# Random-feature attention followed by an ELU layer on one core: the order of work within a beat, the lags of the ELU steps, a PSUM bank of its own for the second products, a fixed pattern of pieces, and x on VectorE

## The chip, the cores and the metric

The kernel runs on one core of one Trainium2 chip. The metric is the device time of one execution in microseconds, median of three runs.

## The reference

```
# attention: q, k, v (8, 8, 576, 64); w_phi (64, 128)
phi(x):  proj = x @ w_phi;  proj -= max(|proj|)
         return concat(exp(proj), exp(-proj))
kv  = phi(k)^T @ v          z = sum over s of phi(k)
x   = phi(q) @ kv / (phi(q) @ z + 1e-6)
# the 8 heads side by side: x is (4608, 512)
h   = x @ w_in              (512 to 2048)
g   = where(h > 0, h, exp(min(h, 0)) - 1)     # ELU
out = g @ w_out             (2048 to 512)
```

## The kernel before

**Attention.** It is cut into 16 quads of four heads (two quads make a batch). One quad's work is a list of steps: transposes of k and q (`tr`), five projections of k (`k_head`: two matmuls into a PSUM tile `pk`, a maximum `m_k` on VectorE, two exponentials `EK` on ScalarE), five of q (`q_head`, only the maximum `m_q`), the scale and six scaled pieces of v on GpSimd (`vs`), five feature products of q (`pq`, two exponentials `Eq`), two `kv` products with a copy by ScalarE, five output heads (`pn0`, `pn1`, combined on VectorE into `tot`), and x = tot times the reciprocal (`rec`), which DMA transposes turn into `xT`. Both exponentials of a `pk` wait for the maximum of the same tile, since the framework orders readers of one PSUM bank. All these PSUM tiles rotate through one pool, `apsum`, of five banks.

**The ELU layer.** It goes in 9 chunks of 512 rows, each of 32 pieces of four 512-column matmuls: 16 first products `mm1` (w_in times xT into `ph`) and 16 second products `mm2` (four 128-row groups `tt`, each of four parts into one bank `po`, then a copy to `o_sb` on ScalarE and a store). Behind each `mm1` come three steps: `e_sb` = exp(ph) on ScalarE, `u_sb` = e - 1 on GpSimd, and `gT` = max(min(u, 0), ph) on VectorE, which gives the bank of `ph` back. `ph` and `po` rotate through one pool, `mpsum`, of three banks. Chunk c needs the xT of batch c; chunk 8 holds the last 64 rows of every head.

**The order.** From quad 2 on each engine's instruction order is the order of the code. Time is cut into slots of 16 beats, one slot for each quad. A slot n holds the k, q and v steps of quad n, the kv and output steps of quad n-1, and the transposes of quad n+1, at beats written out in `slot_beats`. What a step leaves to another engine is put on an agenda by `post(lag, fn)` and is issued at the start of beat now + lag, in the order in which it was posted. A beat issues its agenda, then the attention steps, then as many pieces as a due time asks for (about 10 in a slot up to slot 5, then 16.34). `moe_piece` takes the first products of a chunk while there are no second ones, so that within a chunk the 16 `mm1` come in a row and then the 16 `mm2`. When first and second products of neighbouring chunks stand ready together, they alternate. Quads 0 and 1 come before the beats, in a fixed list.

Of the kernel before, what the change touches and what calls it, by code (L numbers as in the profile page):

```python
# [22 lines left out]
def kernel(  # L23
# [11 lines left out]
    P = 128  # L35
# [87 lines left out]


    beat = [0]
    agenda = {}
    in_beats = [False]

    def post(lag, fn):
        if in_beats[0]:  # L130
            agenda.setdefault(beat[0] + lag, []).append(fn)
# [11 lines left out]
    def attention_steps(i):  # L143
# [57 lines left out]

        def exps(psum, dst):

            for sg in range(2):
                post(
                    1 + sg,
                    lambda sg=sg: nc.scalar.activation(  # L207
# [4 lines left out]
        def k_head(hh):  # L212
            pk = project(st["kT"], hh, st["m_k"])
            if hh < 4:
                exps(pk, lambda sg: st["EK"][:, hh, sg, :])
            else:
                exps(pk, lambda sg: st["EKt"][:, sg, :])

# [30 lines left out]
        def q_features(par, c):  # L249
# [7 lines left out]
            )  # L257
            exps(pq, lambda sg: st["Eq"][:, par, c, sg, :])

        def q_features_tail():  # L260
            pq = apsum.tile([P, 2, P], FP32, name="pq", tag="ap")
            for c in range(2):
# [6 lines left out]
                )  # L269
            exps(pq.rearrange("p a b -> p (a b)"), lambda sg: st["Eqt"][:, sg, :])  # L270

# [3 lines left out]

            post(2, weights)

        def kv(s):
# [17 lines left out]
            for c in range(2):  # L296
                for sg in range(2):
# [7 lines left out]
                    )  # L305
            post(1, lambda: nc.scalar.copy(st["kv"][:, s], pkv))

# [61 lines left out]
        def divide():  # L369
# [4 lines left out]

            def x_head(c):
                r = slice(c * NS, (c + 1) * NS)
                eng.tensor_tensor(  # L377
                    st["x"][:, :, c, :],
# [3 lines left out]
                )  # L382

            for c in range(2):
                post(1 + c, lambda c=c: x_head(c))

# [40 lines left out]
    def mm1(ch, jt):  # L427
# [3 lines left out]
        for ct in range(N_CT):  # L431
# [8 lines left out]
        u_sb = moesm.tile([P, CHUNK], BF16, name="u_sb")  # L440
        post(1, lambda: nc.scalar.activation(e_sb, ph, ACT.Exp))  # L441
        post(
            1,
            lambda: nc.gpsimd.tensor_scalar(  # L444
                u_sb, e_sb, -1.0, 1.0, op0=ALU.add, op1=ALU.mult
            ),
        )
        post(
            2,
            lambda: nc.vector.scalar_tensor_tensor(  # L450
                gTs[ch][:, jt, :], u_sb, 0.0, ph, op0=ALU.min, op1=ALU.max
            ),
        )

    pos = {}

    def mm2(ch, tt, part):

        if part == 0:
            pos[ch, tt] = mpsum.tile([P, DM], FP32, name="po", tag="mp")  # L460
        po = pos[ch, tt]
# [10 lines left out]
        o_sb = moesm.tile([P, DM], FP32, name="o_sb", bufs=2)  # L472
        post(1, lambda: nc.scalar.copy(o_sb, po))  # L473

# [17 lines left out]

    first, second = [], []
    turn = [0]

    def chunk_ready(ch):
        first.extend((ch, jt) for jt in range(N_JT))

    def moe_piece():
        take_first = first and (  # L500
            not second or (turn[0] == 0 and second[0][0] >= first[0][0] - 1)
        )
        if take_first:
            ch, jt = first.pop(0)
            mm1(ch, jt)
            turn[0] = 1
            if jt == N_JT - 1:

                post(
                    2,  # L510
                    lambda: second.extend(
                        (ch, tt, part)
                        for tt in range(CHUNK // P)
                        for part in range(4)
                    ),
                )
        elif second:
            mm2(*second.pop(0))
            turn[0] = 0

# [7 lines left out]
    def slot_beats(n):  # L528
        at = [[] for _ in range(BEATS)]
        old, new, nxt = quads.get(n - 1), quads.get(n), quads.get(n + 1)  # L530
        if n == 2:
            old = None
        if old:
            at[0] += old["kv"][:1]
            at[1] += old["kv"][1:]
            for t, f in zip((3, 5, 7, 9, 11), old["out"]):
                at[t].append(f)
            at[14].append(lambda: post(1, old["x"][0]))
        if new:
            for t, f in zip((0, 1, 3, 4, 5), new["k"]):  # L540
                at[t].append(f)
            for t, f in zip((2, 6, 8, 10, 12), new["q"]):
                at[t].append(f)
            for t, f in zip((7, 9, 11, 13, 15), new["qf"]):
                at[t].append(f)
            at[6].append(lambda: post(1, new["scale"][0]))
            for t, f in zip((7, 8, 9, 10, 11, 11), new["vs"]):
                at[t].append(lambda f=f: post(1, f))
        if nxt:
            at[3] += nxt["tr"][:1]  # L550
            at[6] += nxt["tr"][1:]
        if n % 2 == 1 and n > 3:
            at[4].append(lambda: chunk_ready((n - 3) // 2))
        return at
# [72 lines left out]
    in_beats[0] = True  # L627
    chunk_ready(0)
    done = 0
    for n in range(2, NQ + 1):  # L630
# [3 lines left out]
        if n % 2 == 0 and n // 2 + 1 < B:  # L634
            nb = n // 2 + 1
            alloc_batch(nb)
            for t, f in zip((2, 4, 6, 8), load_kq(nb)):
                at[t].append(f)
            at[10].append(lambda: load_v(nb))
        for t in range(BEATS):  # L640
            next_beat()
            for f in at[t]:
                f()
            now = n + (t + 1) / BEATS
            due = (now - 2) * 32 / 3.25 if now < 5.25 else 32 + (now - 5.25) * 16.34
            while done < due and (first or second):
                moe_piece()
                done += 1
    chunk_ready(B - 1)
    chunk_ready(B)  # L650
    while first or second or agenda:
        next_beat()
# [31 lines left out]
```

## Time and profile before

| | |
|---|---|
| median of 3 runs | 484.35 us (482.02 to 484.66) |
| the profiled execution's own time | 483.06 us |
| its span, first to last instruction | 481.3 us |
| PE (TensorE) busy | 389.0 us, 81% |
| ACT (ScalarE) busy | 270.1 us, 56% |
| DVE (VectorE) busy | 265.8 us, 55% |
| POOL (GpSimd) busy | 244.6 us, 51% |
| mean granted TensorE clock | 0.946 of full speed |

The profile was taken on an execution of 483.06 us, 1.76 us more than its span. Busy times overlap, and a busy TensorE is not TensorE at its peak, since the ends of pipelined matmuls are modelled: how densely it works is read from the distance between the starts of matmuls. PEld is the weight load, which runs beside the matmuls, SPq the queue from which SyncE issues DMAs.

### The profile page before, as it was taken

How to read it: one execution, taken by the hardware profiler on the slowest of the kernel's cores; microseconds unless marked ns; L12 is line 12 of the kernel's file. 1: busy time of each engine (PE TensorE's matmuls, PEld its weight loads, DVE VectorE, ACT ScalarE, POOL GpSimd, SP SyncE). 2: the span in 40 equal slices, each digit the busy share in tenths (PEclk: the TensorE clock that was granted, in tenths of full speed). 3: DMA queues.
4: the chain of work that ended last, by engine and by line, in shares of the span. 5: the costliest groups of instructions: out<-in, count | busy, mean ns of one | idle time of the engine just before them, and what ended most of it. 6: DMA issues, size and time to landing. Idle time of an engine off the chain costs nothing.

```text
span 481.3 us, 7888 instructions
## 1 busy us (share of the span) xinstructions
PE 389.0 (81%) x2888; PEld 206.3 (43%) x2888; DVE 265.8 (55%) x522; ACT 270.1 (56%) x585; POOL 244.6 (51%) x355
## 2 busy tenths in 40 slices
PE   3575757699598797879788977997799779889996
PEld 2344424355244453445344543554355435334442
DVE  2671644578366646664676457745774674264320
ACT  2942156577465666665765657656766683254421
POOL 8645047196166645746393729571925282254320
PEclk9955787899889999999999999999999999999999
DMA  8899974019913981198318930993035003300023
GB/s 132 164 200 199 194 95 63 0 19 152 229 35 51 153 185 47 34 129 201 71 13 117 233 73 1 102 259 72 1 68 98 23 0 49 91 1 22 23 61 69
DMA packets 93718, 44.88 MB, mean 93 GB/s; under 512 B 62544, under 2 KB 88272, under 8 KB 93680
## 3 DMA queue, kind: packets, MB, share of 16 engines
q1 hardware_dynamic: 65136, 29.57, 29.8%
q0 software_dynamic: 28544, 14.82, 23.6%
q8 instruction: 22, 0.36, 0.3%
q14 instruction: 16, 0.13, 0.1%
HBM read 36.77 MB, written 9.44 MB: 96 GB/s over the span
## 4 chain that ended last, share of the span: by engine, by line
PE 37%; POOL 21%; DVE 15%; issue 15%; DMA 7%; ACT 4%; SPq 1%; POOLq 0%; ACTq 0%; DVEq 0%
PE po L463 21%; POOL u_sb L444 12%; PE ph L432 7%; DVE gT L450 6%; DMA q_b<-in_q_dram 3%; POOL vs L242 3%; PE pk L182 3%; POOL x L377 3%; DMA xT<-x 2%; ACT EK L207 2%; DVE tot L337 2%; DVE tot L331 2%; DVE m_q L192 2%; DVE m_k L192 2%; PE pq L251 2%
## 5 line engine op out<-in xcount | busy, mean ns | idle before, releaser
L444 POOL TENSOR_SCALAR u_sb<-e_sb 128x512 bf16<-128x512 f32 x144 | 88.2, 616 | 159.8 <-ACT e_sb L441 144.5
L432 PE MATMUL ph<-xT,w_in_sb 128*128 128x512 bf16 x512 | 134.8, 393 | 38.9 <-DVE gT L450 32.2
L450 DVE SCALAR_TENSOR_TENSOR gT<-u_sb,ph 128x512 bf16<-128x512 bf16 x144 | 97.0, 683 | 115.9 <-POOL u_sb L444 115.1
L463 PE MATMUL po<-w_out_sb,gT 128*128 128x512 bf16 x576 | 140.9, 379 | 0.0
L441 ACT ACTIVATE e_sb<-ph 128x512 f32<-128x512 f32 x144 | 85.4, 602 | 57.7 <-PE ph L432 55.5
L207 ACT ACTIVATE EK<-pk 128x512 bf16<-128x512 f32 x128 | 70.8, 612 | 61.9 <-DVE m_k L192 61.7
L432 PEld LDWEIGHTS <-w_in_sb 128*128 128x128 bf16 x576 | 57.3, 99 | 108.2 <-issue 60.7
L207 ACT ACTIVATE Eq<-pq 128x512 bf16<-128x512 f32 x128 | 73.0, 610 | 21.1 <-PE pq L251 20.9
L463 PEld LDWEIGHTS <-gT 128*128 128x128 bf16 x576 | 55.6, 98 | 53.9 <-issue 1.5
L242 POOL TENSOR_TENSOR vs<-v_b,em 128x512 bf16<-128x512 f32 (+1 forms) x90 | 73.0, 834 | 0.0
L192 DVE TENSOR_REDUCE m_k<-pk 128x4 f32<-128x512 f32 (+1 forms) x80 | 49.1, 632 | 36.8 <-PE pk L182 36.8
L192 DVE TENSOR_REDUCE m_q<-pk 128x4 f32<-128x512 f32 (+1 forms) x80 | 49.9, 627 | 11.0 <-PE pk L182 10.9
L377 POOL TENSOR_TENSOR x<-tot,rec 128x576 bf16<-128x576 f32 x30 | 34.1, 1148 | 16.7 <-DVE rec L373 16.7
L473 ACT COPY o_sb<-po 128x512 f32<-128x512 f32 x36 | 21.3, 590 | 32.2 <-PE po L463 30.2
L182 PE MATMUL pk<-w_phi_both,kT 128*128 128x256 bf16 x144 | 29.5, 288 | 11.3 <-ACT EK L207 6.5
L182 PE MATMUL pk<-w_phi_both,qT 128*128 128x256 bf16 x144 | 30.4, 288 | 7.3 <-ACT EK L207 3.7
L319 PEld LDWEIGHTS <-Eq 128*128 128x128 bf16 x512 | 27.0, 103 | 20.0 <-issue 8.7
L319 PE MATMUL pn<-kv,Eq 128*128 128x65 bf16 x512 | 30.1, 201 | 5.0 <-DVE m_q L192 1.7
L331 DVE TENSOR_TENSOR tot<-pn,w 128x260 f32<-128x260 f32 x64 | 27.0, 423 | 10.2 <-PE pn L319 10.1
L251 PE MATMUL pq<-qT,w_phi_both 128*128 128x512 bf16 x64 | 25.1, 404 | 5.9 <-DVE tot L331 2.1
L337 DVE TENSOR_TENSOR tot<-tot,pn 128x260 f32<-128x260 f32 x64 | 27.0, 424 | 1.9
L182 PEld LDWEIGHTS <-qT 128*128 128x128 bf16 x144 | 14.4, 102 | 25.4 <-issue 13.5
(62 smaller groups left out, 267.2 us busy)
## 6 DMA issues: line engine op xcount, KB each, us to landing
out_dram<-o_sb SPq DMA_DIRECT2D x32, 256.0 KB, 2.7
v_b<-in_v_dram SPq DMA_DIRECT2D x7, 1024.0 KB, 8.7
k_b<-in_k_dram POOLq DMA_DIRECT2D x7, 512.0 KB, 6.1
q_b<-in_q_dram POOLq DMA_DIRECT2D x7, 512.0 KB, 7.8
w_in_sb<-in_moe_w_in_dram POOLq DMA_DIRECT2D x8, 256.0 KB, 8.6
w_out_sb<-in_moe_w_out_dram POOLq DMA_DIRECT2D x8, 256.0 KB, 12.4
v_b<-in_v_dram POOLq DMA_DIRECT2D x2, 512.0 KB, 7.1
out_dram<-o_sb SPq DMA_DIRECT2D x8, 128.0 KB, 2.3
```

What stands on the lines that cost most here:

```text
L182: nc.tensor.matmul(pk[:, 2 * j:2 * j + 2, :].rearrange("p a b -> p (a b)"), xT[:, 2 * hh + j, :], w_phi_rhs, start=True, stop=True,)
L192: lambda: nc.vector.tensor_reduce(m[:, o:o + NT] if hh < 4 else m[:, NS - 1::NS], pk[:, 0:2 * n, :], axis=AX.X, op=ALU.max, apply_absolute ...
L207: lambda sg=sg: nc.scalar.activation(dst(sg), psum, ACT.Exp, scale=1.0 - 2.0 * sg),
L242: eng.tensor_tensor(st["vs"][:, sg, r, 0:D], kqv[b][2][:, o:o + n * D].rearrange("p (n d) -> p n d", d=D), st["em"][:, sg, r, None].to_bro ...
L319: nc.tensor.matmul(pt[:, t, :], st["Eq"][:, par, c, sg, o:o + P], st["kv"][:, s, c, sg, :], start=True, stop=True,)
L331: nc.vector.tensor_tensor(tot, pn[1], st["w"][:, o:o + NT, None].to_broadcast((P, NT, D1)), op=ALU.mult,)
L377: eng.tensor_tensor(st["x"][:, :, c, :], st["tot"][:, r, 0:D], rec[:, r, None].to_broadcast((P, NS, D)), op=ALU.mult,)
L432: nc.tensor.matmul(ph, w_in_sb[:, ct, jt * P:(jt + 1) * P], xTs[ch][:, ct, :] if ch < B else xT_tail[:, ct // 2, :, ct % 2, :], start=(ct ...
L441: post(1, lambda: nc.scalar.activation(e_sb, ph, ACT.Exp))
L444: lambda: nc.gpsimd.tensor_scalar(u_sb, e_sb, -1.0, 1.0, op0=ALU.add, op1=ALU.mult),
L450: lambda: nc.vector.scalar_tensor_tensor(gTs[ch][:, jt, :], u_sb, 0.0, ph, op0=ALU.min, op1=ALU.max),
L463: nc.tensor.matmul(po, gTs[ch][:, jt, tt * P:(tt + 1) * P], w_out_sb[:, jt, :], start=(jt == 0), stop=(jt == N_JT - 1),)
```

## The change

- An agenda item gets a rank; the items of a beat are issued in the order of rank (ELU exponential and u 0, copies from PSUM 1, maxima 2, gT 3, the rest 5, the scale 7).
- The lags of the ELU steps become 1, 2 and 3 beats for `e_sb`, `u_sb` and `gT` (before 1, 1 and 2). Both exponentials of a k projection are posted two beats on, both of a q feature one (before one and two).
- `apsum` has four banks, `mpsum` three for `ph` alone, and a new pool `opsum` one for `po`.
- The pieces stand in a fixed list, one for each beat, issued before the attention steps: two `mm1`, then one `mm2` of the chunk before (its groups 2 and 3), eight times, then the eight `mm2` of the chunk's groups 0 and 1. In chunk 0 the places of the earlier chunk's pieces are empty. A chunk may begin once it is in `ready`, four beats after the issue of its last DMA transposes.
- The steps stand at other beats. Ahead of the beats, x of quad 0 is transposed before the q features of quad 1, and the transposes of quad 2 move to the end.
- x of every quad is multiplied on VectorE, right behind the reciprocal. Before, GpSimd did it one and two beats later (but for quad 1).

```
-        tc.tile_pool(name="apsum", bufs=5, space=bass.MemoryType.PSUM)
+        tc.tile_pool(name="apsum", bufs=4, space=bass.MemoryType.PSUM)
...
+    opsum = ctx.enter_context(
+        tc.tile_pool(name="opsum", bufs=1, space=bass.MemoryType.PSUM)
+    )
...
-    def post(lag, fn):
+    def post(lag, fn, rank=5):
...
-        for fn in agenda.pop(beat[0], []):
+        for _, fn in sorted(agenda.pop(beat[0], []), key=lambda item: item[0]):
             fn()
...
-            def x_head(c):
+            for c in range(2):
                 r = slice(c * NS, (c + 1) * NS)
-                eng.tensor_tensor(
+                nc.vector.tensor_tensor(
...
-        post(1, lambda: nc.scalar.activation(e_sb, ph, ACT.Exp))
+        post(1, lambda: nc.scalar.activation(e_sb, ph, ACT.Exp), 0)
         post(
-            1,
+            2,
             lambda: nc.gpsimd.tensor_scalar(
...
         post(
-            2,
+            3,
             lambda: nc.vector.scalar_tensor_tensor(
...
-            pos[ch, tt] = mpsum.tile([P, DM], FP32, name="po", tag="mp")
+            pos[ch, tt] = opsum.tile([P, DM], FP32, name="po", tag="op")
...
+    for ch in range(B + 1):
+        late = [(ch - 1, tt, part) for tt in (2, 3) for part in range(4)]
+        for j in range(N_JT // 2):
+            pieces += [(ch, 2 * j), (ch, 2 * j + 1)]
+            pieces.append(late[j] if ch > 0 else None)
+        pieces += [(ch, tt, part) for tt in (0, 1) for part in range(4)]
+    pieces += [(B, tt, part) for tt in (2, 3) for part in range(4)]
...
+        if new:
+            put((0, 2, 3, 5, 6), new["k"])
+            at[8].append(lambda: post(1, new["scale"][0], 7))
+            put((9, 10, 11, 12, 13, 14), [lambda f=f: post(1, f) for f in new["vs"]])
         if old:
+            put((3, 4), old["kv"])
+            put((6, 8, 10, 12, 14), old["out"])
+            at[15].append(lambda: post(1, old["x"][0]))
+            if n % 2 == 0:
+                at[15].append(lambda: post(5, lambda: ready.add(n // 2 - 1)))
         if new:
+            put((8, 10, 12, 14, 15), new["qf"])
+            put((0, 2, 9, 11, 14), new["q"])
         if nxt:
+            put((5, 9), nxt["tr"])
...
-    steps += b["vs"][5:] + b["qf"] + quads[2]["tr"]
-    steps += b["kv"] + a["x"] + b["out"] + b["x"]
+    steps += b["vs"][5:] + a["x"] + b["qf"]
+    steps += b["kv"] + b["out"] + b["x"] + quads[2]["tr"]
```

On ScalarE, at the start of slot 2 (the first beats), the order before is this; the number behind a tile's name tells tiles apart:

```order
L207 ACTIVATE EK_501<-pk_664 128x512
L441 ACTIVATE e_sb_673<-ph_668 128x512
L207 ACTIVATE EK_501<-pk_664 128x512
L207 ACTIVATE EK_501<-pk_679 128x512
L441 ACTIVATE e_sb_687<-ph_682 128x512
L207 ACTIVATE EK_501<-pk_679 128x512
```

At the same place on ScalarE the changed kernel has these rows:

```order
L445 ACTIVATE e_sb_673<-ph_668 128x512
L445 ACTIVATE e_sb_689<-ph_684 128x512
L212 ACTIVATE EK_643<-pk_675 128x512 x2
L445 ACTIVATE e_sb_710<-ph_705 128x512
L212 ACTIVATE EK_643<-pk_695 128x512 x2
```

Each `e_sb` stood between the two exponentials of the k projection of its own beat; now it stands ahead of both, and the k projection whose exponentials follow is a beat older.

On VectorE, in the same beats of slot 2, before:

```order
L192 TENSOR_REDUCE m_k_500<-pk_664 128x4
L450 SCALAR_TENSOR_TENSOR gT_667<-u_sb_674,ph_668 128x512
L192 TENSOR_REDUCE m_k_500<-pk_679 128x4
L450 SCALAR_TENSOR_TENSOR gT_667<-u_sb_688,ph_682 128x512
L192 TENSOR_REDUCE m_q_517<-pk_695 128x4
```

On VectorE in the changed kernel:

```order
L196 TENSOR_REDUCE m_k_642<-pk_675 128x4
L196 TENSOR_REDUCE m_q_659<-pk_678 128x4
L196 TENSOR_REDUCE m_k_642<-pk_695 128x4
L196 TENSOR_REDUCE m_q_659<-pk_698 128x4
L455 SCALAR_TENSOR_TENSOR gT_667<-u_sb_674,ph_668 128x512
L196 TENSOR_REDUCE m_k_642<-pk_712 128x4
L455 SCALAR_TENSOR_TENSOR gT_667<-u_sb_690,ph_684 128x512
```

The first `gT` stood behind one maximum; now four maxima, of two later projections of k and two of q, stand ahead of it.

GpSimd before, at the end of slot 5 (`u_sb` of chunk 1, x of quad 4):

```order
L242 TENSOR_TENSOR vs_1598<-v_b_663,em_1595 128x2x64 x2
L444 TENSOR_SCALAR u_sb_1703<-e_sb_1702 128x512
L377 TENSOR_TENSOR x_1498<-tot_1497,rec_1708 128x9x64
L444 TENSOR_SCALAR u_sb_1724<-e_sb_1723 128x512
L377 TENSOR_TENSOR x_1498<-tot_1497,rec_1708 128x9x64
```

VectorE in the changed kernel, at the end of slot 5, x of quad 4:

```order
L196 TENSOR_REDUCE m_q_1576<-pk_1674 128x2
L365 TENSOR_TENSOR tot_1506<-pnt_1663,w_1406 128x2x65
L371 TENSOR_TENSOR tot_1506<-tot_1506,pnt_1663 128x2x65
L379 TENSOR_SCALAR den_1682<-tot_1506 128x18
L380 RECIPROCAL rec_1683<-den_1682 128x18
L384 TENSOR_TENSOR x_1507<-tot_1506,rec_1683 128x9x64 x2
L455 SCALAR_TENSOR_TENSOR gT_1447<-u_sb_1652,ph_1646 128x512
```

x has left GpSimd, where it stood between two `u_sb`; on VectorE it now stands between the reciprocal and the next `gT`.

## Rows read from the trace of the kernel before

**Rows 1.** Stretch, length, busy time (count) of PE, PEld, DVE, ACT, POOL; PEclk, DMA share, GB/s.

```profile
55.40:130.00 74.60, 55.56 (x419) 29.39 (x418) 42.01 (x79) 45.70 (x102) 37.74 (x53) 0.89 0.67 100
130.00:417.70 287.70, 246.53 (x1934) 130.65 (x1934) 173.38 (x343) 176.85 (x388) 156.67 (x221) 0.99 0.49 88
163.30:179.90 16.60, 16.60 (x147) 9.36 (x146) 8.04 (x18) 11.44 (x27) 8.44 (x11) 1.00 1.04 195
179.90:208.60 28.70, 21.43 (x170) 11.27 (x169) 17.99 (x36) 18.98 (x42) 16.32 (x25) 1.00 0.25 53
```

**Rows 2.** Waits of the engines: us in total, times, longest us.

```profile
DVE gT L450 <- POOL u_sb L444: 115.1, 101, 7.5
...
PE ph L432 <- DVE gT L450: 32.3, 47, 2.0
```

**Rows 3.** Timeline of slot 2: start us, us, engine, instruction, idle before it.

```profile
57.35 0.60 ACT L441 ACTIVATE e_sb<-ph 128x512 f32<-128x512 f32 x1
58.04 0.61 POOL L444 TENSOR_SCALAR u_sb<-e_sb 128x512 bf16<-128x512 f32 x1 [11.28 <-ACT e_sb L441]
58.69 0.69 DVE L450 SCALAR_TENSOR_TENSOR gT<-u_sb,ph 128x512 bf16<-128x512 bf16 x1 [2.15 <-POOL u_sb L444]
59.29 0.68 DVE L192 TENSOR_REDUCE m_k<-pk 128x4 f32<-128x512 f32 x1
60.01 0.60 ACT L207 ACTIVATE EK<-pk 128x512 bf16<-128x512 f32 x1 [1.57 <-DVE m_k L192]
60.50 0.59 ACT L441 ACTIVATE e_sb<-ph 128x512 f32<-128x512 f32 x1
```

**Rows 4.** Timeline of TensorE where only second products run beside attention.

```profile
163.33 1.02 PE L463 MATMUL po<-w_out_sb,gT 128*128 128x512 bf16 x4
164.19 0.41 PE L319 MATMUL pn<-kv,Eq 128*128 128x65 bf16 x8
164.43 0.38 PE L251 MATMUL pq<-qT,w_phi_both 128*128 128x512 bf16 x1
164.65 1.02 PE L463 MATMUL po<-w_out_sb,gT 128*128 128x512 bf16 x4
...
174.34 0.67 PE L286 MATMUL pkv<-vs,EK 128*128 128x65 bf16 x16
...
175.17 0.39 PE L182 MATMUL pk<-w_phi_both,kT 128*128 128x256 bf16 x2
175.40 1.03 PE L463 MATMUL po<-w_out_sb,gT 128*128 128x512 bf16 x4
```

**Rows 5.** Groups by line: busy us, mean ns of one, idle before.

```profile
L306 ACT CAST kv<-pkv 128x260 bf16<-128x260 f32 x32 | 12.3, 396 | 10.0 <-PE pkv L298 9.7
...
L377 DVE TENSOR_TENSOR x<-tot,rec 128x576 bf16<-128x576 f32 x2 | 1.4, 754 | 0.0
```

**Rows 6.** Timeline of GpSimd and VectorE late in slot 4.

```profile
115.75 3.78 POOL L242 TENSOR_TENSOR vs<-v_b,em 128x512 bf16<-128x512 f32 x5
...
116.87 1.99 DVE L372 TENSOR_SCALAR den<-tot 128x18 f32<-128x18 f32 x1
```

**Rows 7.** Timeline of the last stretch, chunks 7 and 8.

```profile
424.09 2.75 PE L432 MATMUL ph<-xT,w_in_sb 128*128 128x512 bf16 x12 [0.44 <-DVE gT L450]
...
442.02 1.03 PE L432 MATMUL ph<-xT_tail,w_in_sb 128*128 128x512 bf16 x4
442.22 0.58 ACT L473 COPY o_sb<-po 128x512 f32<-128x512 f32 x1 [0.21 <-PE po L463]
...
475.69 1.03 PE L463 MATMUL po<-w_out_sb,gT 128*128 128x512 bf16 x4
```

**Rows 8.** Timeline of the opening, ahead of the beats.

```profile
36.02 0.27 DVE L373 RECIPROCAL rec<-den 128x18 f32<-128x18 f32 x1
...
42.12 1.03 PE L156 MATMUL tr<-ident,q_b 128*128 128x128 bf16 x8 [2.67 <-DMA q_b<-in_q_dram]
```

**Rows 9.** Timeline of TensorE at the start of chunk 1.

```profile
130.46 2.72 PE L432 MATMUL ph<-xT,w_in_sb 128*128 128x512 bf16 x6 [4.85 <-DMA xT<-x]
```

More of the change, by code (lines that the diff above doesn't have):

```diff
@@ L127 @@
     in_beats = [False]
-    def post(lag, fn):
+    def post(lag, fn, rank=5):
         if in_beats[0]:
-            agenda.setdefault(beat[0] + lag, []).append(fn)
+            agenda.setdefault(beat[0] + lag, []).append((rank, fn))
         else:
@@ L198, in project, with exps @@
                 ),
+                2,
             )
             return pk[:, 0:2 * n, :].rearrange("p a b -> p (a b)")
-        def exps(psum, dst):
+        def exps(psum, dst, lag):
             for sg in range(2):
                 post(
-                    1 + sg,
+                    lag,
                     lambda sg=sg: nc.scalar.activation(
@@ L214, in k_head @@
             if hh < 4:
-                exps(pk, lambda sg: st["EK"][:, hh, sg, :])
+                exps(pk, lambda sg: st["EK"][:, hh, sg, :], 2)
             else:
-                exps(pk, lambda sg: st["EKt"][:, sg, :])
+                exps(pk, lambda sg: st["EKt"][:, sg, :], 2)
         def q_head(hh):
@@ L257, in q_features @@
             )
-            exps(pq, lambda sg: st["Eq"][:, par, c, sg, :])
+            exps(pq, lambda sg: st["Eq"][:, par, c, sg, :], 1)
         def q_features_tail():
@@ L269, in q_features_tail @@
                 )
-            exps(pq.rearrange("p a b -> p (a b)"), lambda sg: st["Eqt"][:, sg, :])
+            exps(
+                pq.rearrange("p a b -> p (a b)"), lambda sg: st["Eqt"][:, sg, :], 1
+            )
             def weights():
@@ L274, in weights @@
                 nc.scalar.activation(st["w"], st["m_q"], ACT.Exp, scale=2.0)
-            post(2, weights)
+            post(2, weights, 6)
         def kv(s):
@@ L305, in kv @@
                     )
-            post(1, lambda: nc.scalar.copy(st["kv"][:, s], pkv))
+            post(1, lambda: nc.scalar.copy(st["kv"][:, s], pkv), 1)
         def out_head(hh):
@@ L382, in x_head @@
                 )
-            for c in range(2):
-                post(1 + c, lambda c=c: x_head(c))
         def x_out():
@@ L440, in mm1 @@
         u_sb = moesm.tile([P, CHUNK], BF16, name="u_sb")
-        post(1, lambda: nc.scalar.activation(e_sb, ph, ACT.Exp))
+        post(1, lambda: nc.scalar.activation(e_sb, ph, ACT.Exp), 0)
         post(
-            1,
+            2,
             lambda: nc.gpsimd.tensor_scalar(
@@ L446, in mm1 @@
             ),
+            0,
         )
         post(
-            2,
+            3,
             lambda: nc.vector.scalar_tensor_tensor(
@@ L452, in mm1 @@
             ),
+            3,
         )
@@ L472, in mm2 @@
         o_sb = moesm.tile([P, DM], FP32, name="o_sb", bufs=2)
-        post(1, lambda: nc.scalar.copy(o_sb, po))
+        post(1, lambda: nc.scalar.copy(o_sb, po), 1)
         def store():
@@ L489, in mm2 @@
         post(2, store)
[L493 to L497, printed above, removed]
-    def moe_piece():
[L500 to L519, printed above, removed]
+    ready = set()
+    pieces = []
+    for ch in range(B + 1):
[5 more added lines that the diff above has]
+    pieces += [(B, tt, part) for tt in (2, 3) for part in range(4)]
+    def moe_piece():
+        if not pieces or (pieces[0] and pieces[0][0] not in ready):
+            return
+        piece = pieces.pop(0)
+        if piece:
+            (mm1 if len(piece) == 2 else mm2)(*piece)
     quads = {}
@@ L532, in slot_beats, with put @@
             old = None
-        if old:
[L534 to L538, printed above, removed]
-        if new:
[L540 to L548, printed above, removed]
+        def put(beats, fs):
+            for t, f in zip(beats, fs):
+                at[t].append(f)
+        if new:
+            put((0, 2, 3, 5, 6), new["k"])
+            at[8].append(lambda: post(1, new["scale"][0], 7))
+            put((9, 10, 11, 12, 13, 14), [lambda f=f: post(1, f) for f in new["vs"]])
+        if old:
+            put((3, 4), old["kv"])
[3 more added lines that the diff above has]
+                at[15].append(lambda: post(5, lambda: ready.add(n // 2 - 1)))
+        if new:
+            put((8, 10, 12, 14, 15), new["qf"])
+            put((0, 2, 9, 11, 14), new["q"])
         if nxt:
[L550 to L553, printed above, removed]
+            put((5, 9), nxt["tr"])
         return at
@@ L627 @@
     in_beats[0] = True
-    chunk_ready(0)
-    done = 0
+    ready.add(0)
     for n in range(2, NQ + 1):
@@ L636 @@
             alloc_batch(nb)
-            for t, f in zip((2, 4, 6, 8), load_kq(nb)):
+            for t, f in zip((4, 5, 6, 7), load_kq(nb)):
                 at[t].append(f)
-            at[10].append(lambda: load_v(nb))
+            at[6].append(lambda: load_v(nb))
         for t in range(BEATS):
             next_beat()
+            moe_piece()
             for f in at[t]:
                 f()
[L644 to L651, printed above, removed]
+    while pieces or agenda:
+        if B - 1 in ready:
+            ready.add(B)
         next_beat()
```

## The prediction

> **What bounds the kernel now.** I read the busy time by stretch first. Between 130.0 us, where chunk 1 begins to flow, and 417.7 us, where chunk 7 does, six chunks pass in 287.7 us, 47.95 us each [rows 1]. No engine is full there: PE 246.5, ACT 176.9, DVE 173.4 us. Within one chunk there are two regimes. In the 16.6 us from 163.3, which hold only second products, PE is busy throughout at full clock; in the 28.7 us from 179.9, which hold the 16 first products, it is busy 21.4 [rows 1]. So PE does not limit a chunk, the first products do.
>
> The waits say by what: DVE waits 115.1 us for u_sb, and PE 32.3 us, in 47 waits, for a gT to give a bank of ph back [rows 2]. The timeline of slot 2 shows why no one is full [rows 3]. An e_sb starts at 57.35, its u_sb at 58.04, its gT at 58.69; only behind that gT may DVE take the maximum of the next k projection (59.29), only behind that maximum may ACT start its exponentials (60.01), and the next e_sb stands behind the first of these (60.50). That is a ring through three engines, 3.15 us a turn, one first product per turn, where PE's own work for such a product is 0.86. In the drain nothing else runs, but three banks for ph are too few for a run of first products alone: after every twelve matmuls PE waits 0.44 [rows 7].
>
> **What the changed order leaves as PE's own work.** The prices come from the stretch in which PE never waits, as distances between starts [rows 4]. A piece of four matmuls takes 0.86 (163.33 to 164.19), an output head 0.24, a q feature 0.22, a kv product 0.83 (174.34 to 175.17), two projection matmuls 0.23. A quad has two kv products (1.66), four heads and a tail counted as one (1.20), 18 projection matmuls (2.07), four features and a small one (0.99): 5.9 us. A chunk has 32 pieces and spans two slots, so 27.6 + 11.8 = 39.4 us. The other engines: DVE spent 173.4 / 6 = 28.9 per chunk and gets the two x, 3.0 more, so 31.9; ACT stays at 29.5. Both are under 39.4, so PE can become the bound if the order lets it.
>
> **Ranks, lags and pattern.** With e_sb first in its beat, u_sb one beat later and gT two beats later behind the maxima, no step waits in its queue behind another that waits for it: the ring is open. I walked one pair of slots beat by beat with the prices above and those of the other engines: an exponential or e_sb starts 0.49 behind the last one (60.01 to 60.50), a gT holds DVE 0.60 (58.69 to 59.29) [rows 3]. What is left per chunk:
>
> Four banks in apsum: the second kv product takes the bank of the second k projection, whose exponentials are issued in the same beat on ACT, behind the copy of the first kv product (mean 0.396 [rows 5]). The copy and two exponentials need about 1.55 with their hand-overs, the piece that hides them is 0.86: PE waits 0.7 in each slot, with all its later work behind, 1.4. Likewise one pn tile waits for the last k exponentials, 0.3 a slot, 0.6.
>
> One bank for po: PE may start the next row group only after the copy. At 442.02 the next product started, the copy at 442.22, for 0.58 [rows 7]; with a hand-over back 0.85. Before, that cost nothing, since two more banks covered it. Of a chunk's four group changes two have other pieces between, two do not; there 0.1 to 0.2 of attention hides some: 1.4.
>
> x on DVE: 0.754 each, two per quad [rows 5]. On GpSimd it stood between u_sb. On DVE it stands in beat 15 behind den and rec, and ahead of a gT. A maximum (0.35), combines, den and rec (1.1), both x (1.5) and that gT (0.6) make some 3.7 us after beat 14; PE needs the gT's bank after 2.3 (a piece, 0.11, a piece, 0.44). PE waits 1.5 there, in one of the two slots of a chunk; in the other slot no first product follows.
>
> The ph ring itself: three banks, but of each three pieces only two take one, so a bank is due back after four pieces, 3.44. The measured turn is 3.19 (2.75 + 0.44 [rows 7]), so no wait in the drain; among the maxima I count 0.4 per chunk.
>
> One more for x: a den, an operation on 18 columns, took 1.99 us while five GpSimd multiplications ran in a row [rows 6]; the reciprocal of the same 18 columns takes 0.27 [rows 8]. So some DVE instructions stand still while GpSimd runs. For x, bounds are 0 (GpSimd idle just then) and one whole GpSimd instruction for each, two times 1.0. I take 0.8 per chunk, a u_sb and a bit, since by beat 15 the long vs pieces are done.
>
> The rule of the Trainium skill for this is in "SBUF — State Buffer", section "Who interferes with whom": a VectorE instruction with two SBUF inputs, as this multiplication has, and a GpSimd instruction that reads SBUF exclude each other for a whole instruction. The den agrees, though no row shows it for x beside GpSimd. By that rule the upper bound holds, and a chunk loses 2.1 instead of 0.8.
>
> Sum: 39.4 + 1.4 + 0.6 + 1.4 + 1.5 + 0.4 + 0.8 = 45.5 us per chunk. The sixth chunk spans slot 16, which has no new quad: it lacks 3.1 of PE's work and 1.0 of the waits, 41.4. Six chunks: 5 x 45.5 + 41.4 = 268.9, against 287.7.
>
> The DMA issues of k and q on GpSimd move from beats 2 to 8 into 4 to 7; they stand between u_sb that have a beat to spare, which hides them. Without that beat each of the four would hold a u_sb, and a gT, for its length. On SP the transposes of q now stand behind the load of v: rival (b).
>
> **The opening.** Before, PE stood in the fixed list in front of transposes that wait for q_b (2.67 idle at 42.12 [rows 8]), with kv, x and the outputs of quad 1 behind them. These transposes move to the end. But now x of quad 0 stands ahead of quad 1's q features: rec starts at 36.02 [rows 8], x ends at 37.8, and transposes, features, ten exponentials and kv follow one another, so that quad 1's outputs begin near 45 and the end of the list comes near 55. I count no gain: 55.4 stays.
>
> From 55.4 to chunk 1 it took 74.6 us, with the ring at its worst and the clock at 0.89 [rows 1]. Now chunk 0 has one beat per piece. Slot 2: 11 first products and three us of attention, PE 12.5, and ACT 27 exponentials of 0.49 plus small ones, 15; I take 17. Slot 3: 13 pieces and 5.9 are 17.1, with 1.8 of the waits above 19. Slot 4 and the first four beats of slot 5 hold no piece at all. Slot 4 is then bound by DVE and ACT, 10 to 12, and by a clock that may fall: I take 15. Until chunk 1 flows another 8.5 pass, since its xT leaves only at the end of slot 4; before, PE waited 4.85 for it [rows 9]. Together 59.5: chunk 1 at 114.9.
>
> **The drain.** Before, 63.6 us from 417.7 to the end of the span, 481.3, with 64 pieces. Now the last eight pieces of chunk 6 are mixed in: 72 x 0.86 = 61.9. Nothing hides the po copies: six group changes of 0.85, 5.1. Behind the last product, which ends near 476.55 (475.69 + 0.86 [rows 7]), copy and store took 4.75 and will again. 71.8, that is 8.2 more.
>
> **The sum.** 114.9 + 268.9 + 71.8 = 455.6 us of span. The profiled execution was 483.06, 1.76 above its span: 457.4. The median shown is 1.29 above that execution, so I predict 459 us, 5% faster.
>
> **Rivals.** (a) *The period stays.* If waits that I don't see take what the open ring frees, a chunk keeps 47.95: 114.9 + 287.7 + 71.8, with the same additions 477.5. For it: in the dense stretch of 16.6 us there are no ELU steps, so no row shows PE and ELU dense together beside attention. Against: DVE and ACT have over 7 us to spare in each chunk. Chance 0.10.
>
> (b) *DMA becomes the bound.* Loads for the next batch now go out in four beats of even slots, and the transposes of q behind them must land before beat 0 of the next slot. At chunk 1 PE waited 4.85 for a transpose [rows 9], in a window that moved 195 GB/s the DMA share was 1.04 [rows 1]. Three us lost in each of six even slots: 477. Chance 0.10.
>
> (c) *x and GpSimd exclude each other fully.* 1.3 more per chunk, 8 in all: 467. The den of 1.99 [rows 6] shows that it can be. Chance 0.08.
>
> (d) *Slower: the short rings.* Four banks for attention, 26 tiles a slot, and PE in order: if three more tiles per slot wait for exponentials of their own beat as the second kv product does, at 0.7 each, 14 slots lose 29 us: 488. The gain is gone from 2.6 such tiles on. For it: the dense stretch that gave the prices [rows 4] ran with five banks. Against: by the walk most tiles have two beats between release and need. Chance 0.09.
>
> (e) *The clock falls in the empty stretch* of 20 beats and chunk 0 runs at 1.2 GHz as it partly does now (0.89 granted): 5 to 8 us, 465. Chance 0.05.
>
> The forecast keeps 0.58; its own range is 449 to 468. The range that leaves out no more than 2 in 10 reaches to (a) and (b): 447 to 479. About 0.5% is what a measurement of this kernel can tell from no change: faster 0.87, same 0.04, slower 0.09.
>
> **What would show it.** Right: starts of first products of neighbouring chunks 44 to 47 us apart; DVE's wait for u_sb below half of 115.1; waits of PE for o_sb near 0.6 to 0.9, some 20 in number; a wait of PE for gT in the beats behind an x; the first ph of chunk 1 near 115; drain near 72. Wrong: PE waits for DMA in even slots (b); x of well over 0.754 (c); frequent waits of PE for ACT exponentials (d); a low clock in slot 4 (e).

## The result and the profile after

The changed kernel takes 445.49 us (median of 4 runs, 444.58 to 447.8) against 483.19 (4 runs, 482.02 to 484.66). The ratio is 0.923, 95% interval 0.918 to 0.928: 7.7% faster, where 5% was predicted. 445.49 lies 1.5 us under the predicted range. The profiled execution took 446.22 us, its span is 444.4.

Busy time by stretch, with the same columns as [rows 1]: from the first beat to chunk 1, inside that slot 4 and the lead to chunk 1, then the six chunks, one steady chunk, and the drain.

```profile
55.09:113.75 58.66, 44.90 (x355) 24.88 (x354) 42.19 (x80) 40.66 (x93) 33.04 (x49) 0.88 0.81 117
92.06:106.70 14.64, 9.73 (x107) 5.93 (x105) 11.32 (x24) 10.56 (x27) 5.63 (x8) 0.82 1.22 206
106.70:113.75 7.05, 3.70 (x30) 2.42 (x30) 5.56 (x11) 2.20 (x6) 1.19 (x3) 0.50 0.94 125
113.75:372.19 258.44, 238.88 (x1964) 129.60 (x1963) 189.57 (x370) 176.81 (x394) 132.31 (x197) 1.00 0.56 96
247.58:291.11 43.53, 40.51 (x342) 22.26 (x339) 33.04 (x64) 31.22 (x72) 24.31 (x36) 1.00 0.68 122
372.19:444.40 72.21, 63.45 (x289) 28.04 (x287) 22.02 (x32) 25.54 (x43) 19.75 (x32) 0.99 0.15 45
```

Six chunks now pass in 258.4 us instead of 287.7 and PE is busy for 92% of that; the opening stretch went from 74.6 to 58.7; the drain grew from 63.6 to 72.2. The waits of the whole span, as in [rows 2]:

```profile
DVE gT L455 <- POOL u_sb L448: 43.2, 46, 9.6
PE ph L436 <- DVE gT L455: 15.4, 18, 2.0
PE po L469 <- ACT o_sb L479: 12.2, 19, 0.7
PE pk L186 <- DMA qT<-q_b: 4.3, 2, 3.3
```

VectorE's wait for u_sb fell from 115.1 to 43.2 and PE's for gT from 32.3 to 15.4; PE's wait for the copy of po is new. Two places of a steady chunk, on the timeline. First the end of the slot, where x stands (start us, us, engine, instruction, idle before it):

```profile
261.15 0.40 POOL L247 TENSOR_TENSOR vs<-v_b,em 128x128 bf16<-128x128 f32 x1
261.23 0.36 DVE L379 TENSOR_SCALAR den<-tot 128x18 f32<-128x18 f32 x1
261.52 0.62 POOL L448 TENSOR_SCALAR u_sb<-e_sb 128x512 bf16<-128x512 f32 x1
...
261.92 1.49 DVE L384 TENSOR_TENSOR x<-tot,rec 128x576 bf16<-128x576 f32 x2
...
262.10 0.38 PE L186 MATMUL pk<-w_phi_both,qT 128*128 128x256 bf16 x2
...
262.83 1.05 POOL L448 TENSOR_SCALAR u_sb<-e_sb 128x512 bf16<-128x512 f32 x1 [0.70 <-ACT e_sb L445]
263.33 0.68 DVE L455 SCALAR_TENSOR_TENSOR gT<-u_sb,ph 128x512 bf16<-128x512 bf16 x1
...
264.06 1.02 PE L436 MATMUL ph<-xT,w_in_sb 128*128 128x512 bf16 x4 [1.58 <-DVE gT L455]
```

The two x last 1.49 together, as cheap as predicted; the gT behind them comes late and PE waits 1.58 for it by the profile's list. Counted between starts, as the prediction's prices are, it is 1.74: the two projection matmuls of 262.10 take 0.22, so PE could go on at 262.32 and does at 264.06. Then the two kv products:

```profile
245.41 0.67 PE L293 MATMUL pkv<-vs,EK 128*128 128x65 bf16 x16
...
246.62 1.09 ACT L212 ACTIVATE EK<-pk 128x512 bf16<-128x512 f32 x2
...
247.11 0.67 PE L293 MATMUL pkv<-vs,EK 128*128 128x65 bf16 x16
```

The second product starts at 247.11, while the exponentials of the second k projection still run (246.62 to 247.71; they are the second pair of this slot on ScalarE). It does not wait for them, and the prediction had it wait 0.7 there. In the drain, the rows that answer to [rows 7]:

```profile
394.00 3.61 PE L469 MATMUL po<-w_out_sb,gT 128*128 128x512 bf16 x16 [0.67 <-ACT o_sb L479]
398.28 1.89 PE L469 MATMUL po<-w_out_sb,gT 128*128 128x512 bf16 x8 [0.67 <-ACT o_sb L479]
```

The 16 products from 394.00 are 3.44 of work (four take 0.86), and the next row group starts 4.28 after them: the copy of po costs 0.84 there, where 0.85 was predicted.

### The profile page after: what moved, and what is told of

Its sections match the earlier page's. It is cut to its first block, busy times and chain, and to the rows that moved or that the text cites. A ratio compares the mean times of both kernels' runs of the same rounds, so it can differ in the third digit from the quotient of the medians.

```text
span 444.4 us, 7930 instructions
## 1 busy us (share of the span) xinstructions
PE 378.0 (85%) x2888; PEld 203.7 (46%) x2888; DVE 284.5 (64%) x552; ACT 266.7 (60%) x585; POOL 213.3 (48%) x325
## 4 chain that ended last, share of the span: by engine, by line
PE 63%; DVE 13%; ACT 11%; DMA 5%; issue 4%; POOL 3%; POOLq 0%; ACTq 0%
PE ph L436 24%; PE po L469 23%; PE pk L186 5%; ACT Eq L212 4%; PE pkv L293 4%; DMA qT<-q_b 4%; DVE x L384 3%; ACT EK L212 3%; DVE gT L455 3%; PE pq L256 2%; ACT o_sb L479 2%; PE pn L326 2%; PE pkv L305 1%; DVE m_q L196 1%; DVE m_k L196 1%
## 5 line engine op out<-in xcount | busy, mean ns | idle before, releaser
L448 POOL TENSOR_SCALAR u_sb<-e_sb 128x512 bf16<-128x512 f32 x144 | 91.4, 636 | 161.9 <-ACT e_sb L445 155.6
L469 PE MATMUL po<-w_out_sb,gT 128*128 128x512 bf16 x576 | 142.4, 379 | 12.2 <-ACT o_sb L479 12.2
L436 PE MATMUL ph<-xT,w_in_sb 128*128 128x512 bf16 x512 | 131.6, 384 | 15.8 <-DVE gT L455 15.4
L445 ACT ACTIVATE e_sb<-ph 128x512 f32<-128x512 f32 x144 | 87.0, 606 | 68.0 <-PE ph L436 65.8
L455 DVE SCALAR_TENSOR_TENSOR gT<-u_sb,ph 128x512 bf16<-128x512 bf16 x144 | 97.4, 682 | 44.0 <-POOL u_sb L448 43.2
L469 PEld LDWEIGHTS <-gT 128*128 128x128 bf16 x576 | 55.4, 98 | 70.2 <-issue 16.1
L436 PEld LDWEIGHTS <-w_in_sb 128*128 128x128 bf16 x576 | 54.3, 98 | 71.1 <-issue 23.5
L212 ACT ACTIVATE Eq<-pq 128x512 bf16<-128x512 f32 x128 | 68.9, 605 | 29.6 <-PE pq L256 29.0
L196 DVE TENSOR_REDUCE m_k<-pk 128x4 f32<-128x512 f32 (+1 forms) x80 | 50.3, 635 | 45.0 <-PE pk L186 44.8
L326 PE MATMUL pn<-kv,Eq 128*128 128x65 bf16 x512 | 28.6, 199 | 3.1 <-DVE tot L338 1.3
L293 PEld LDWEIGHTS <-EK 128*128 128x128 bf16 x512 | 21.6, 102 | 6.7 <-ACT EK L212 2.3
L186 PEld LDWEIGHTS <-kT 128*128 128x128 bf16 x144 | 14.7, 103 | 20.0 <-issue 6.5
```

What stands on the lines that cost most here:

```text
L186: nc.tensor.matmul(pk[:, 2 * j:2 * j + 2, :].rearrange("p a b -> p (a b)"), xT[:, 2 * hh + j, :], w_phi_rhs, start=True, stop=True,)
L196: lambda: nc.vector.tensor_reduce(m[:, o:o + NT] if hh < 4 else m[:, NS - 1::NS], pk[:, 0:2 * n, :], axis=AX.X, op=ALU.max, apply_absolute ...
L212: lambda sg=sg: nc.scalar.activation(dst(sg), psum, ACT.Exp, scale=1.0 - 2.0 * sg),
L293: nc.tensor.matmul(pkv[:, c, sg, :], st["EK"][:, 2 * c + s, sg, t * F:(t + 1) * F], st["vs"][:, sg, c * NS + s * NT + t, :], start=first, ...
L326: nc.tensor.matmul(pt[:, t, :], st["Eq"][:, par, c, sg, o:o + P], st["kv"][:, s, c, sg, :], start=True, stop=True,)
L436: nc.tensor.matmul(ph, w_in_sb[:, ct, jt * P:(jt + 1) * P], xTs[ch][:, ct, :] if ch < B else xT_tail[:, ct // 2, :, ct % 2, :], start=(ct ...
```

## The experiments

The theory: the ring of e_sb, u_sb, gT, maximum and exponentials set the period, and ranks with lags opened it. The rival: the fixed 2:1 pattern (two first products, then one second product) made the gain. "Distance" below is that from the first e_sb of one steady chunk to that of the next, read from the timeline (43.5 in the kernel after, 48.4 in that before). The edits are against the kernel after, unless said otherwise.

**The order of the steps and the order of the pieces.** Five kernels separate them. Without both ranks and longer lags:

```diff
-        for _, fn in sorted(agenda.pop(beat[0], []), key=lambda item: item[0]):
+        for _, fn in agenda.pop(beat[0], []):
...  u_sb
-            2,
+            1,
...  gT
-            3,
+            2,
...  exps
-                    lag,
+                    1 + sg,
```

> The kernel after, with the order of the ELU steps as before: no ranks in a beat, u_sb one beat and gT two beats behind the first product, the two exponentials one and two beats behind. The pattern of pieces, the banks and x on VectorE stay as after. Theory (the ring through e_sb, u_sb, gT, maximum, exponentials was the bound, and ranks with lags opened it): the ring is closed again, VectorE waits over 100 us for u_sb instead of 43, a chunk takes 47 to 49 us instead of 43.5, and the whole 468 to 480 us. Rival (the fixed pattern, which spreads the first products over both slots, is what frees the time): chunks stay at 43.5 to 44.5 and the whole under 453 us.

Measured 461.22 us (460.28 to 462.31). Its waits and one chunk:

```profile
DVE gT L455 <- POOL u_sb L448: 103.3, 93, 9.6
ACT EK L212 <- DVE m_k L196: 43.9, 41, 2.1
```

```profile
258.48:304.76 46.28, 41.07 (x333) 22.34 (x336) 32.60 (x64) 31.17 (x71) 23.87 (x36) 1.00 0.66 113
```

The ring is closed again, as the wait of 103.3 shows, but it costs 2.8 us a chunk and 15.7 in all, less than expected: more than half of the gain over 483 stays. So neither theory nor rival had it alone. Next the first line of that diff by itself (lags without ranks), and the middle two by themselves (ranks without the lags of u_sb and gT).

> The kernel after, with the longer lags but without the ranks: within a beat the steps go out in the order in which they were posted. Theory: the lags give a u_sb and a gT a beat to spare each, so about half of the gain of the order stays: chunks of 44.5 to 46, the whole 452 to 460 us. If the ranks carry it all: 468 or more; if the lags alone do: 445 to 448.

> The kernel after, with the ranks but with u_sb one beat and gT two beats behind the first product, as before; the exponentials keep their new lags. Theory: gT stands behind two maxima while its u_sb has just begun, and VectorE waits for it in most beats: VectorE's wait for u_sb 70 to 100 us, chunks of 45 to 47, the whole 455 to 466 us. Rival (ranks alone do it): 445 to 448.

Without ranks: 437.65 us (437.15 to 438.35), *faster* than the kernel after by 7.8; distance 42.4. With ranks and old lags: 444.0 (443.56 to 444.26), distance 43.2. Their waits for u_sb, in this order:

```profile
DVE gT L455 <- POOL u_sb L448: 48.1, 55, 9.6
DVE gT L455 <- POOL u_sb L448: 50.5, 59, 9.6
```

Each of the two opens the ring, and having both is worse than the lags alone. Both kernels keep the later exponentials, which the first one had put back; no run has these alone, so their share is open. Then the pieces, with ranks and lags kept:

```diff
-        late = [(ch - 1, tt, part) for tt in (2, 3) for part in range(4)]
-        for j in range(N_JT // 2):
-            pieces += [(ch, 2 * j), (ch, 2 * j + 1)]
-            pieces.append(late[j] if ch > 0 else None)
-        pieces += [(ch, tt, part) for tt in (0, 1) for part in range(4)]
-    pieces += [(B, tt, part) for tt in (2, 3) for part in range(4)]
+        pieces += [(ch, jt) for jt in range(N_JT)]
+        pieces += [(ch, tt, part) for tt in range(4) for part in range(4)]
```

> The kernel after, with the 16 first products of a chunk in a row and then its 16 second products, nothing mixed; ranks, lags, banks and x on VectorE stay. Theory (order of the steps, not the pattern): the slot with first products is bound by VectorE (16 gT of 0.6 and the attention's 11 to 12 us, 21 to 22), the other by TensorE (13.8, 5.9 and copies of po, 21), so chunks of 43.5 to 46, the whole 447 to 460 us. Rival (the pattern makes the gain): chunks near 48, 470 us or more.

Measured 527.24 us (522.12 to 528.03): slower than the kernel before by 8.7% (ratio 1.087, 1.082 to 1.093). The theory as I held it falls here. PE's waits in one chunk of 57.3 us (in one of 54.4 they are much the same, 11.1 for gT):

```profile
PE ph L436 <- DVE gT L455: 10.7, 9, 2.0
PE po L469 <- ACT o_sb L479: 1.9, 3, 0.7
```

The timeline shows one such wait:

```profile
243.96 0.38 PE L186 MATMUL pk<-w_phi_both,qT 128*128 128x256 bf16 x2
...
244.38 0.69 DVE L196 TENSOR_REDUCE m_q<-pk 128x4 f32<-128x512 f32 x1 [0.41 <-PE pk L186]
...
244.98 1.28 DVE L455 SCALAR_TENSOR_TENSOR gT<-u_sb,ph 128x512 bf16<-128x512 bf16 x2
...
245.72 1.02 PE L436 MATMUL ph<-xT,w_in_sb 128*128 128x512 bf16 x4 [1.38 <-DVE gT L455]
```

The gT that returns the bank, three beats old, stands behind the maximum of a projection that PE has only just made (243.96), so PE's projection, maximum, gT and PE's next first product follow one another: a new ring. The row shows the part of the ranks in it: VectorE waits 0.41 for that projection, and by its rank gT stands behind that maximum, where it would stand ahead of it in the order of posting. The part of the longer lag is argued and not shown: three banks hold three beats of first products and no more, so a gT three beats on leaves no beat to spare. No run has pieces in a row with the lags alone or the ranks alone. With a second product among each three pieces PE has other work there. Old lags and no ranks together with the clumped pieces:

> The 16 first products of a chunk in a row and then its 16 second products, and with that the old lags and no ranks; banks, x on VectorE and the places of the attention steps stay as after. With the new lags and ranks this order of pieces took 527 us. Theory (the longer lags hold a bank of ph for a beat more, which only the 2:1 pattern can afford; with the old lags the clumped order is as good as the kernel before): chunks of 47 to 51, the whole 475 to 495 us. Rival (the clumped order alone makes the loss, whatever the lags): 515 us or more. Rival (the pattern gives nothing with the old order of steps): 461 us, as the pattern with the old lags had.

Measured 477.27 us (476.95 to 477.57), distance 47.7. The four corners:

| | pieces in a row | 2:1 pattern |
|---|---|---|
| old lags, no ranks | 477.27 us, distance 47.7 | 461.22 us, distance 46.3 |
| new lags and ranks | 527.24 us, distance 54 to 57 | 445.49 us, distance 43.5 |

The first corner is within 6 us of the kernel before. From there the pattern alone gives 16, the order of the steps alone loses 50, and the order on top of the pattern gives 15.7: the two edits have to be priced together. No run takes back the places of the attention steps or the own bank of po alone; the first corner has both of these edits.

**x on VectorE.**

```diff
-            for c in range(2):
+            def x_head(c):
                 r = slice(c * NS, (c + 1) * NS)
-                nc.vector.tensor_tensor(
+                eng.tensor_tensor(
...
+            for c in range(2):
+                post(1 + c, lambda c=c: x_head(c))
...
-            at[15].append(lambda: post(1, old["x"][0]))
+            at[15].append(lambda: post(3, old["x"][0]))
```

> The kernel after, with the two multiplications x of a quad back on GpSimd, one and two beats behind the divide, and the transposes of x two beats later, so that they stand behind x. Ranks, lags, pattern and banks stay. Theory (x on VectorE costs TensorE a wait of 1.58 us for the gT behind it once a chunk): that wait goes, but x takes 1.15 on GpSimd between u_sb and xT comes two beats later, for which TensorE waits 1 to 3 us at the start of a chunk: chunks of 43.0 to 45.0, the whole 443 to 452 us. Rival (x on VectorE carries much of the gain, since GpSimd would hold u_sb back): 456 or more. Rival (x on VectorE is a pure loss): 436 or less.

Measured 449.95 us (448.53 to 453.35), in the expected range for another reason. A chunk is 42.2, 1.3 shorter, and a wait of PE for xT appears only once, for 1.0. But the first e_sb of the beats starts at 62.4 instead of 55.3. On the opening's timeline GpSimd stands on issues of weight loads, x of quad 0 behind them, and PE behind x:

```profile
40.71 1.41 POOL L86 DMA_DIRECT2D w_out_sb<-in_moe_w_out_dram  x2 [4.55 <-DMA q_b<-in_q_dram]
43.15 0.71 POOL L86 DMA_DIRECT2D w_out_sb<-in_moe_w_out_dram  x1 [1.02 <-DMA q_b<-in_q_dram]
43.88 2.26 POOL L384 TENSOR_TENSOR x<-tot,rec 128x576 bf16<-128x576 f32 x2
...
46.20 1.03 PE L408 MATMUL tr<-ident,x 128*128 128x128 bf16 x8 [10.67 <-POOL x L384]
```

So x on VectorE is worth 7 us once, in the opening, and costs 1.3 in each chunk. The stretch from there to chunk 1 is 3.3 longer with x on GpSimd, with waits of PE for kT (3.90) and qT (5.33) in it.

**The opening's list.**

```diff
-    steps += b["vs"][5:] + a["x"] + b["qf"]
-    steps += b["kv"] + b["out"] + b["x"] + quads[2]["tr"]
+    steps += b["vs"][5:] + b["qf"] + quads[2]["tr"]
+    steps += b["kv"] + a["x"] + b["out"] + b["x"]
```

> The kernel after, with the opening's list of steps in the order of before: the transposes of q for quad 2 ahead of kv, and x of quad 0 behind kv. Nothing else differs. Theory (what the new list saves in one place it loses in the other): the first beat starts within 1 us of the 55.1 of after, the whole 444.5 to 447 us. Rival (the wait of 2.67 for q_b comes back whole): 448 us.

Measured 451.27 us (449.9 to 456.89). Without the execution of 456.89 the median is 450.12, 4.6 slower than after and above both expectations, so the new list is worth something once x is on VectorE. The execution of 456.89 is the profiled one, so only its opening is read here: PE waits 3.73 and 2.07 us for q_b there, against 2.67 in [rows 8]. Why q_b came later was not settled.

**Banks.**

```diff
-        tc.tile_pool(name="apsum", bufs=4, space=bass.MemoryType.PSUM)
+        tc.tile_pool(name="apsum", bufs=3, space=bass.MemoryType.PSUM)
...
-        tc.tile_pool(name="opsum", bufs=1, space=bass.MemoryType.PSUM)
+        tc.tile_pool(name="opsum", bufs=2, space=bass.MemoryType.PSUM)
```

> The kernel after, with one bank moved from the attention tiles to the second products: three and two instead of four and one. Theory (four banks are enough because every tile finds a bank released a beat before, three are not, since an output head then gets the bank of the fourth k projection, whose exponentials come two beats later): the waits of TensorE for the copy of po, 12.2 us in all, go, but each slot loses 2 to 4 us to waits for ScalarE's exponentials, chunks of 46 to 50, the whole 460 to 490 us. Rival (the attention banks have slack to give): chunks of 42.3, the whole 432 to 438 us.

Measured 457.31 us (456.42 to 458.1), distance 45.5. The copies of po cost nothing any more (the drain, from its first e_sb, takes 65.7 instead of 70.8), but in a chunk PE now waits for attention's exponentials:

```profile
PE pn L326 <- ACT EK L212: 2.3, 2, 1.5
PE ph L436 <- DVE gT L455: 1.4, 1, 1.4
PE pq L256 <- ACT EKt L212: 0.4, 2, 0.2
```

Rival (d) of the prediction is real at three banks (2.3 a chunk for the output heads) and absent at four.

**Which rank.** Three kernels change one rank each: gT ahead of the maxima, the maxima without a rank, e_sb without a rank.

```diff
...  gT
-            3,
+            1,
```

> The kernel after with one number changed: gT has rank 1 instead of 3, so that it goes ahead of the maxima of its beat. All else stays, the other ranks too. It is to say why the kernel without ranks took 437.65 us and the one with ranks 445.5. Theory (the harm is the gT behind the maxima: a bank of ph comes back two maxima, 1.2 us, later): most of the 7.8 us come, the whole 437 to 440 us, chunks of 42.4 to 42.8. Rival (the harm is e_sb ahead of the exponentials, or the small ones at the end of the beat): 444 to 446.

> The kernel after with the maxima at the rank that a step has without one, so that they go out behind gT and among the combines as posted; the ranks of e_sb, u_sb, gT, copies and small ones stay. Theory (the last maximum of a slot, of 0.4 us, goes ahead of the combine, den, rec and x by its rank, and each maximum ahead of a combine holds an output bank): most of the 7.8 us that the ranks cost, the whole 437 to 440 us. Rival (the harm is on ScalarE, e_sb ahead of the exponentials): 444 to 446.

> The kernel after with e_sb at the rank that a step has without one, so that it goes out among the exponentials of its beat as posted, behind those posted earlier; all other ranks stay. Theory (the harm of the ranks is on VectorE): 444 to 448 us. Rival (e_sb ahead of the exponentials holds the banks of attention and so TensorE): 437 to 441.

Measured 445.54 (444.07 to 447.41), 449.84 (448.26 to 451.68) and 448.98 us (447.99 to 451.2). None gives the 7.8 us back, and the last two are 4.4 and 3.5 slower than the kernel after: all three theories of one bad rank fall. What can be read is that the last maximum of a slot stands ahead of den and x with the ranks and behind them without, and that PE's wait behind x is 1.58 with the ranks and 1.14 without. That is 0.44 of the 1.1 us a chunk; a wait for gT of 0.16 comes with the ranks too, and the rest is in no listed wait. Which ranks act together stays open.

**A better version.** On the kernel without ranks: every other row group of the drain in one of the idle attention banks; x on VectorE for quads 0 and 1 alone, on GpSimd afterwards; both.

```diff
-            pos[ch, tt] = opsum.tile([P, DM], FP32, name="po", tag="op")
+            if ch >= B - 1 and tt % 2:
+                pos[ch, tt] = apsum.tile([P, DM], FP32, name="po", tag="ap")
+            else:
+                pos[ch, tt] = opsum.tile([P, DM], FP32, name="po", tag="op")
...
-                nc.vector.tensor_tensor(
+                (nc.vector if i < 2 else eng).tensor_tensor(
```

> The kernel without ranks (437.65 us), and from chunk 7 on every other row group of second products takes one of the attention banks, which are idle there. Theory (each group change of the drain costs the copy of po, and a second bank hides it, as the two banks of the run with three and two did: 65.7 instead of 70.8 us from the first e_sb of chunk 7 on): 5 us less, 431.5 to 434 us. Rival (the drain is bound by the ring of ph or by the stores behind): 436.5 or more.

> The kernel without ranks (437.65 us), with x on VectorE for quads 0 and 1 alone and on GpSimd, one and two beats behind the divide, for all later ones. Theory (x on VectorE is worth its 7 us in the opening, where GpSimd is full, and costs one wait of 1.1 us a chunk afterwards): 6 times 1.1 less, 430 to 434 us, chunks of 41.3 to 42.0. Rival (without ranks the gT no longer suffers from x, or the later xT takes it back): 436 or more.

> Both of the last two changes together, without ranks: the attention banks for every other row group in the drain, and x on GpSimd from quad 2 on. If the two gains add, as different stretches should: 425 to 429 us.

Measured 434.11 (433.6 to 434.71), 434.9 (433.92 to 435.85) and 430.68 us (430.26 to 431.36; ratio to before 0.891, 0.889 to 0.893). Each of the three falls a little short of its expectation, but the gains of 3.5 and 2.75 add up (together 7.0). This is the fastest version of this study. The drain gained 4.2, not 5. With x on GpSimd a chunk is 41.25, but chunk 1 starts 2.0 later. One chunk of the last kernel, and all the waits of PE that the profile lists in it:

```profile
242.23:283.48 41.25, 40.02 (x339) 22.14 (x336) 29.68 (x60) 30.90 (x71) 28.23 (x40) 1.00 0.73 127
```

```profile
PE po L475 <- ACT o_sb L485: 1.2, 2, 0.7
```

## Why the prediction was right in direction and short in size

**The step that failed is the sum of the waits left in a chunk: 6.1 us predicted, 3.8 measured, so that a chunk takes 43.5 and not 45.5.** Term by term:

| per chunk | predicted | measured |
|---|---|---|
| PE's own work | 39.4 | 39.7 (41.25 - 1.55, the last kernel above) |
| second kv product behind exponentials | 1.4 | 0 |
| output tile behind the last k exponentials | 0.6 | 0 |
| copy of po | 1.4 | 1.55 (1.2 listed) |
| gT behind x | 1.5 | 1.74 (1.58 listed) |
| ring of ph among maxima | 0.4 | 0.33 (0.16 listed) |
| x beside GpSimd | 0.8 | 0.06, and 0.18 for den, both inside the 1.74 |
| not found | - | 0.2 (the rest to 43.5) |

The waits are counted between starts, like the prices of the prediction; the profile's list, with its modelled ends of matmuls, has each of the four 0.16 shorter.

Two sizes were wrong. The first is 2.0 us for "four banks in apsum": it measured 0. I had assumed that banks are handed out in turn, so that the second kv product gets the bank of the second k projection. The bank numbers in the built program say otherwise (they are read from the program; no trace shows them):

```
second k projection   bank 2
second q projection   bank 3
third k projection    bank 0
first kv product      bank 1
second kv product     bank 3
```

By these it gets the bank of the second *q* projection, which VectorE's maximum had freed before. What the trace shows is that it starts at 247.11, under the exponentials, so it does not have their bank. That bank numbers had to be read instead of assumed is the lesson of this case. With three banks a wait for exponentials is there (2.3 a chunk), but of the output heads, not of the kv product. For the output tile that I had priced at 0.6 a chunk no bank number is at hand; no such wait stands in the steady chunk.

The second is 0.8 for x beside GpSimd. The exclusion exists, but GpSimd paid most of it (the timeline above): x took 1.49 for two and the u_sb beside it 1.05 instead of 0.62, and nothing waited for that u_sb: the gT for which PE was waiting started the moment x ended. In the other slot of a chunk, where GpSimd stands idle, den and x of the same kernel take:

```profile
240.35 0.18 DVE L379 TENSOR_SCALAR den<-tot 128x18 f32<-128x18 f32 x1
...
240.86 1.43 DVE L384 TENSOR_TENSOR x<-tot,rec 128x576 bf16<-128x576 f32 x2
```

So x lost 0.06 to GpSimd, behind a u_sb that had begun 0.40 earlier, and the den of 0.36 lost 0.18, behind the multiplication of 261.15. Where a u_sb had started just before x, in the kernel with the maxima unranked, VectorE paid:

```profile
260.70 1.41 POOL L246 TENSOR_TENSOR vs<-v_b,em 128x512 bf16<-128x512 f32 x2
...
262.02 0.70 DVE L378 TENSOR_SCALAR den<-tot 128x18 f32<-128x18 f32 x1
262.07 0.62 POOL L447 TENSOR_SCALAR u_sb<-e_sb 128x512 bf16<-128x512 f32 x1
...
263.03 0.62 POOL L447 TENSOR_SCALAR u_sb<-e_sb 128x512 bf16<-128x512 f32 x1
263.06 1.86 DVE L383 TENSOR_TENSOR x<-tot,rec 128x576 bf16<-128x576 f32 x2
```

There x takes 1.86 instead of 1.43, and PE's wait behind x is 2.0. The rule of the Trainium skill ("SBUF — State Buffer", section "Who interferes with whom") says that the one that issues first keeps the shared ports for its whole instruction and the other is blocked. Both rows of x agree: 0.43 more for the u_sb in the one, 0.43 more for x in the other. The den of 0.70 was not first either: GpSimd had been at its multiplications since 260.70, and the den ended at 262.72, just behind the u_sb that followed them (262.69).

**The other terms.** Six chunks: 268.9 predicted, 258.4 measured; the sixth 41.4 against 38.9, the first two 44.3 and 44.7, the second with a wait of 0.99 for qT. Opening: chunk 1 at 114.9 predicted, 113.75 measured, slot by slot 17, 19, 15 and 8.5 predicted against 18.7, 18.3, 14.6 and 7.05. That the opening itself would not move was right (55.09 after 55.4), but as a sum: without the new list the whole takes 4.6 longer, and without x on VectorE the opening 7. Drain: 71.8 against 72.2. Span: 455.6 against 444.4, of which 10.5 are the chunks. The last 2.3 of the 13.5 us between 459 and 445.49 are what I added to the span for the execution and the median (3.4; it was 1.1).

**The mechanism** was half right. The ring did bind, and its waits fell as foretold. But I gave the credit to ranks and lags together and treated the pattern as a detail of the ring of ph. The corners above show that lags and ranks without the pattern lose 50 us, and that the ranks on top of the lags lose 7.8.

**The rivals.** (a) fell: distance 43.5, not 47.95. (b) appeared twice, 4.3 us in all and 3.3 of them ahead of chunk 1, not in every even slot. (c) is the exclusion above; 0.06 of x was on PE's path, the rest on GpSimd. The prediction counts the den as a case of it; the den has one tensor input and not two like x, and its rows above show only that it waited for GpSimd too. (d) is true of three banks, not of four. (e) came, inside the sum: in slot 4 the clock granted was 0.82, and after that slot, in which PE was busy 9.7 of 14.6 us, it was 0.50 until chunk 1, the lower level of 1.2 GHz; my 15 and 8.5 covered it.

## What to carry to other kernels

Read which bank a tile really gets before pricing a wait for it; a pool need not hand them out in turn. Price the order of the steps and the order of the pieces together, since the same lags and ranks lost 50 us here with the first products in a row and gained 15.7 with other work in between; and when an order is made of two devices (lags and ranks), try each alone. An operation that moves to another engine can be right in the opening and wrong in the steady state: split it there.

## What was not expected of the hardware

That the exclusion costs whole tenths on the engine that nobody waits for: GpSimd's u_sb took 1.05 us instead of 0.62 beside x on VectorE, while with x on GpSimd (the kernel with x there from quad 2 on) none of 42 u_sb between 200 and 300 us took over 0.65.
